# Channel loop of a gated attention and S4 backward kernel: the parameter rows move to the front of an iteration and get a third buffer, the lag sums change their PSUM bank

## The chip, the cores and the metric

The kernel runs on one core of one Trainium2 chip. The metric is the device time of one execution in microseconds (us). Three runs are shown; the profile is of a further execution with a time of its own.

## The reference

The reference is the forward pass of a block and the gradients of all its inputs but one. The block mixes, row by row of x (2048 rows of 576 channels, bfloat16), an attention with 32 heads of width 18 and a convolution of S4 kind with 128 complex states per channel:

```python
x = A_x
g = _sigmoid((x * gate_w).sum(-1, keepdims=True))
a = _A_ref(x, A_wqkv, A_wo)          # softmax attention, 32 heads
b = _B_ref(x, B_A_re, B_A_im, B_B_re, B_B_im, B_C_re, B_C_im, B_log_dt, B_Dskip)
return g * a + (1 - g) * b
...
# _B_ref: K[d,l] = Re sum_n C[d,n] exp(dt[d] A[d,n] l) dB[d,n];  y = causal convolution of K and u, + u * Dskip
_out, _vjp = jax.vjp(_f, A_x, A_wqkv, A_wo, B_A_re, B_A_im, B_B_re, B_B_im, B_C_re, B_C_im, B_log_dt, B_Dskip, gate_w)
```

So thirteen outputs are written: the result, and the gradients of x, the two attention weights, six S4 matrices of 576 x 128, two vectors of the S4 part and the gate.

## The kernel before, in words

The program has four stages that follow each other: projections and preparation, attention forward and backward (8 groups of 4 heads), the channel loop, and a final stage of weight gradients and row-wise outputs. Only the channel loop is changed. It starts at about 2141 us of the profiled execution and ends at about 2587 us.

**The channel loop** (lines 1412 to 1470) does the S4 forward and backward for 576 channels in 18 blocks of CB = 32. It is a software pipeline: iteration i finishes block i, runs the first half of the state scan of block i+1, prepares block i+2 (called sb) and loads for block i+3 (called mb). The order of the instructions is written out by hand on every engine, and SyncE's DMA queue is one of these engines: what stands first in the code is issued first, and an instruction that waits holds up all that stand behind it on its engine.

In one iteration, in the order of the code:

- `scan` (710, on DVE): seven steps over the states of two blocks at once. The first operation of a step multiplies the state by the parameter rows (`tz<-HG,par`, 727). Before it `scan_open` (704) casts the first column out of UV. In iteration i the second of the two chains needs the rows of block i+1.
- `rw1`, `rw2` (744, 751, DVE): products over the whole scan, which read the parameter rows of block i for the last time and leave Rw.
- `m_sum(sb)` (637, PE): four pairs of small matmuls that sum skewed rows (skw) into 32 columns of PSUM, the lag sums, `misc<-sel,skw`. `m_fin(sb)` (642, ACT) copies them out, the third copy into `dDs_row`.
- `m_part(mb)` (611): 32 matmuls (`psM<-xs,gyp`), two copies to mst on ACT (621), and two stores of 288 KB to the DRAM tensor Md_d (622). `m_load(mb+1)` (604) then loads xs (1 MB) and gyp.
- `turn_e(sb, 0)` (655): transposes of the first half of the basis E1n, copied to E1e by ACT.
- `k0(i+1)`, `k0_out` (761, 772): a column sum on PE, a copy K0c on ACT, a store of 8 KB to Kp_d (776). `t0_load(i+1)` (848) reads 1 MB back from Kp_d as T0w (854), so it waits for that store.
- `uv(sb, 0)`, `t0(i)`: matmuls. `m_skw(mb)` (629): four loads of 64 KB (635) that read Md_d with a skew.
- `turn_e(sb, 1)`, then **`load_par(sb)`** (668): three loads of 64 KB, each of 512 rows of 128 bytes, that bring the parameter rows of block i+2. There are two buffers (tag par), and so the rows of block i+2 take the buffer of block i.
- `ybp(i, 0)`, `ybp(i, 1)` (787, PE): matmuls on Rw. Around them `load_en(mb, 0)` and `load_en(mb, 1)` (678): two loads of 1 MB of E1n, each into the buffer that `ybp(i, h)` has just read. `uv(sb, 1)` stands between them.
- `prep_rx` (ACT), `load_rx` every second iteration (RXn, two loads of 256 KB in rows of 128 bytes), `yd_out` (ACT, and every second iteration a store of 512 KB in rows of 128 bytes).
- `pairs1`, `pairs2` (DVE products pq, summed by PE into PSUM with `psum`, 813), `wk_cast(sb)` (ACT, reads the parameter rows), `sums` (841: ACT copies the 384 columns out as `m<-misc`, 843; GpSimd combines them).

**The two banks of sums.** misc2 holds two PSUM tiles of one bank each (lines 1370 to 1373). The bank of block b is b % 2. Columns 0 to 383 take the pair sums of `psum`, 384 to 415 the lag sums (`dkp`, 624), 416 to 447 those of `k0`. `dkp(b)` uses the other bank, (b + 1) % 2. In iteration i the lag sums of block i+2 so fall into bank (i+1) % 2, which is the bank of block i-1, whose pair sums ACT copies out at the end of iteration i-1. In the built program the first matmul of the lag sums waits for that copy, although the two touch other columns; the copies and matmuls of one bank wait for each other as a whole.

**Memory.** The parameter rows lie in a pool on the right side that is opened near the end of the attention stage. `dDs_row` (1347) is one row of 576 float32 in a pool of the channel stage; the final stage converts it to bfloat16 (1634).

Of the kernel before, what the change touches and what calls it, by code (L numbers as in the profile page):

```python
# [11 lines left out]
BF = mybir.dt.bfloat16  # L12
F32 = mybir.dt.float32
# [4 lines left out]
P = 128  # L18


def build(tc, aps, dbg_aps=None, stages=("s1", "attn", "post", "s4", "final")):
# [40 lines left out]
    with ExitStack() as gctx:  # L62
# [559 lines left out]
            Q["mdma"](Md_d[d0 + u * 16:d0 + (u + 1) * 16].rearrange("(q g) t w -> (g t) q w", g=4), mst)  # L622

        def dkp(b):
            return Q["misc2"][(b + 1) % 2][:, 12 * CB:13 * CB]

        skws = {}

# [39 lines left out]
        def load_par(b, dma=nc.sync.dma_start):  # L668
            if b == NBLK - 1:
                par = Q["pw"].tile([P, XB, NCOL], BF, tag="RX", bufs=2, name="par_l").bitcast(F32)[:, 0:12, :]  # L670
            else:
                par = Q["pl"].tile([P, 12, CB], F32, tag="par", bufs=2, name="par")
            blk(b)["par"] = par
            for s_ in range(2):
                dma(par[:, s_:8:2, :], par_d[:, 0:4, b * CB:(b + 1) * CB])
            dma(par[:, 8:12, :], par_d[:, 4:8, b * CB:(b + 1) * CB])
# [58 lines left out]
        def cast1(b, nm, s_):  # L735
            B_ = blk(b)
            HGv = B_["HG"].rearrange("p (r s) k c -> p r s k c", s=2)
            B_[nm] = Q["pw"].tile([P, 2, NS, CB], BF, tag=nm, name=nm)
            nc.scalar.copy(B_[nm], HGv[:, :, s_, ::-1, :])
# [602 lines left out]
        if "s4" in stages:  # L1342
            s4c_cm = tc.tile_pool(name="s4c", reuse_waits="tile", bufs=1)
            s4c = s4c_cm.__enter__()
            SS = Q["SS"] = s4c.tile([P, 6, D], F32, name="SS")
            CK = Q["CK"] = s4c.tile([P, 2, 2, D], BF, name="CK")
            dDs_row = Q["dDs_row"] = s4c.tile([1, D], F32, name="dDs_row")
            ones_f = s4c.tile([P, 1], BF, name="ones_f")
            nc.vector.memset(ones_f, 1.0)

            with ExitStack() as ctx:
                pc = ctx.enter_context(tc.tile_pool(name="s4l", reuse_waits="tile", bufs=1))
                pw = Q["pw"] = Q["en", 2] = ctx.enter_context(tc.tile_pool(name="s4lw", reuse_waits="tile", bufs=1))
                Q["ple"] = ctx.enter_context(tc.tile_pool(name="s4le", reuse_waits="tile", bufs=1))
                pps = Q["ps"] = ctx.enter_context(tc.tile_pool(name="s4lps", reuse_waits="tile", bufs=1, space=bass.MemoryType.PSUM))
                pidx_i = pc.tile([P, 1], mybir.dt.int32, name="pidx_i")
                nc.gpsimd.iota(pidx_i, pattern=[[0, 1]], base=0, channel_multiplier=1)
                l0col = pc.tile([P, 1], F32, name="l0col")
                nc.vector.tensor_copy(l0col, pidx_i)
                l1col = pc.tile([P, 1], F32, name="l1col")  # L1360
                nc.vector.tensor_scalar(l1col, l0col, 1.0, None, op0=A.add)
                sel = pc.tile([P, NSUB], F32, name="sel")
                nc.gpsimd.memset(sel, 1.0)
                nc.gpsimd.affine_select(out=sel, in_=sel, compare_op=A.is_ge, fill=0.0,
                                        base=0, pattern=[[-SUB, NSUB]], channel_multiplier=1)
                nc.gpsimd.affine_select(out=sel, in_=sel, compare_op=A.is_ge, fill=0.0,
                                        base=SUB - 1, pattern=[[SUB, NSUB]], channel_multiplier=-1)
                Q["l0col"], Q["l1col"], Q["sel"] = l0col, l1col, sel
                Q["psM"] = lambda: pps.tile([P, 4, P], F32, tag="bk", bufs=4, name="psM")
                misc2 = Q["misc2"] = []  # L1370
                for u in range(2):
                    m_u = pps.tile([P, 512], F32, tag=f"misc{u}", name=f"misc{u}")
                    misc2.append(m_u)

                ctx.enter_context(tc.manual_schedule(engines={mybir.EngineType.PE, mybir.EngineType.Activation, mybir.EngineType.DVE, mybir.EngineType.Pool}))
                dve_copy = nc.vector.tensor_copy
                KH = NS // 2 + 1
                with tc.manual_schedule(engines={mybir.EngineType.SP}):
                    prep_rx(0, dve_copy)
                    load_en(2, 0)  # L1380
                    wk_cast(0)
                    k0(0)
                    k0_out(0)
                    t0_load(0)
                    turn_e(0, 0, 0, 4, dve_copy)
                    m_sum(0)
                    m_fin(0)
                    uv(0, 0)
                    prep_rx(1, dve_copy)
                    load_rx(1)  # L1390
                    turn_e(0, 1, 0, 4, dve_copy)
                    m_part(1, 0)
                    m_part(1, 1)
                    m_skw(1)
                    m_load(2)
                    uv(0, 1)
                    turn_e(1, 0, 0, 4, dve_copy)
                    scan_open(0)
                    scan((0, 1, KH, 0), (0, 1, KH, 1))
                    turn_e(1, 1, 0, 4)  # L1400
                    m_sum(1)
                    m_fin(1)
                    load_en(2, 1)
                    uv(1, 0)
                    m_part(2, 0)
                    m_part(2, 1)
                    m_skw(2)
                    uv(1, 1)
                    m_load(3)
                    prep_rx(2)  # L1410
                    wk_cast(1)
                    for i in range(NBLK):
                        nx = i + 1 < NBLK
                        mb = i + 3 if i + 3 < NBLK else None
                        sb = i + 2 if i + 2 < NBLK else None
                        if nx:
                            scan_open(i + 1)
                            scan((i, KH, NS, None), (i + 1, 1, KH, None))
                        else:
                            scan((i, KH, NS, 0), (i, KH, NS, 1))  # L1420
                        rw1(i)
                        rw2_open(i)
                        rw2(i)
                        if sb is not None:
                            m_sum(sb)
                            m_fin(sb)
                        if mb is not None:
                            m_part(mb, 0)
                            m_part(mb, 1)
                            if mb + 1 < NBLK:  # L1430
                                m_load(mb + 1)
                        if sb is not None:
                            turn_e(sb, 0, 0, 4)
                        if nx:
                            k0(i + 1)
                        if nx:
                            k0_out(i + 1)
                        cast1(i, "hR", 0)
                        nc.scalar.copy(Q["CK"][:, :, :, i * CB:(i + 1) * CB], BK[i]["UV"][:, :, CDK:CDK + 2, :])
                        if sb is not None:  # L1440
                            uv(sb, 0)
                        t0(i, 0)
                        t0(i, 1)
                        if nx:
                            t0_load(i + 1)
                        cast1(i, "gR", 1)
                        if mb is not None:
                            m_skw(mb)
                        if sb is not None:
                            turn_e(sb, 1, 0, 4)  # L1450
                            load_par(sb)
                        ybp(i, 0)
                        if mb is not None:
                            load_en(mb, 0)
                        if sb is not None:
                            uv(sb, 1)
                        ybp(i, 1)
                        if mb is not None:
                            load_en(mb, 1)
                            prep_rx(mb)  # L1460
                            if mb % 2 == 1 and mb + 1 < NBLK:
                                load_rx((mb + 1) // 2)
                        yd_out(i, 0)
                        yd_out(i, 1)
                        pairs1(i)
                        pairs2(i)
                        if sb is not None:
                            wk_cast(sb)
                        sums(i)
                        BK.pop(i)  # L1470
# [298 lines left out]
```

## Time and profile before

| what | value |
|---|---|
| median of three runs | 2766.22 us (2761.52 to 2767.05) |
| profiled execution, time / span | 2764.32 us / 2762.6 us |
| busy in the span: PE, DVE, ACT, POOL | 88%, 83%, 85%, 62% |
| granted TensorE clock | 0.952 |
| start of an iteration's scan (cast out of UV), i = 0 and i = 17 | 2141.5 us, and 2544.5 us for the last block (a scan is opened an iteration ahead) |
| DVE waits for the parameter rows | 39.0 us, 15 times, 5.3 us the longest |
| PE waits for the copy `m<-misc` before the lag sums | 20.5 us, 16 times |

The profiled execution took 1.7 us more than its span, and 1.9 us less than the median. Times in the text are microseconds from the start of the span. A row of the timeline has the start, the time taken, the engine (SPq is SyncE's DMA queue), the line, the operation with output and input, and in brackets the idle time before it and what ended that. A row of the waits has the engine and line that waited, on what, the sum, how often and the longest.

### The profile page before, as it was taken

Reading aid. Unit: us, or ns where it says so; the run is one execution under the profiler, and the core shown is the slowest. Engines: PE = TensorE matmul, PEld = TensorE weight load, DVE = VectorE, ACT = ScalarE, POOL = GpSimd, SP = SyncE. Lnnn points to the kernel's source line nnn. Section 1 sums busy time; section 2 is a strip of 40 time slices with the busy share of each in tenths; the row PEclk is TensorE's granted clock in tenths of the full one; section 3 lists DMA queues with packets and bytes.
Section 4 is the critical chain, followed back from the end, with each engine's and each line's share of the span. In section 5 each row is a group of like instructions: output and inputs, shape, how many; then the busy total and the mean of one; then the engine's idle time right before and its main releaser. Section 6 shows DMA issues by size and latency. Waiting matters only on the chain. (4 is left out here: it accounts for less than half of the span.)

```text
span 2762.6 us, 70109 instructions
## 1 busy us (share of the span) xinstructions
PE 2430.1 (88%) x27411; PEld 1159.8 (42%) x27411; DVE 2301.0 (83%) x4141; ACT 2360.2 (85%) x2744; POOL 1715.3 (62%) x2667
## 2 busy tenths in 40 slices
PE   8898889898899898889898899898886888888789
PEld 4433333333333333333333333332324788887557
DVE  5649999999899998899999999998973888889944
ACT  5489999999999999999999999999963788887121
POOL 0278878888988888788888888879411133332010
PEclk9889999999999999999999999999966899999899
DMA  7647799989889888988997897796789889885996
GB/s 226 181 108 153 156 173 172 159 159 190 155 163 177 169 157 169 169 163 156 179 166 152 162 183 156 152 190 146 139 165 209 214 239 246 221 239 166 249 261 133
DMA packets 1268279, 491.96 MB, mean 178 GB/s; under 512 B 1161765, under 2 KB 1238166, under 8 KB 1259242
## 3 DMA queue, kind: packets, MB, share of 16 engines
q1 hardware_dynamic: 1231466, 414.96, 73.3%
q0 software_dynamic: 23120, 59.76, 8.6%
q10 hardware_dynamic: 13360, 12.75, 1.6%
q8 instruction: 215, 3.52, 0.6%
q14 instruction: 118, 0.97, 0.1%
HBM read 146.86 MB, written 98.52 MB: 89 GB/s over the span
## 5 line engine op out<-in xcount | busy, mean ns | idle before, releaser
L1321 DVE TENSOR_TENSOR ds<-ps_P,PT 128x512 bf16<-128x512 f32 x2048 | 1311.0, 682 | 128.1 <-PE ps_P L30 87.8
L1316 ACT ACTIVATE eb<-ps_P 128x1024 bf16<-128x1024 f32 x1024 | 1100.9, 1075 | 38.2 <-PE ps_P L30 38.0
L1311 ACT ACTIVATE PT<-ps_P 128x1024 bf16<-128x1024 f32 x1024 | 1106.2, 1081 | 19.9 <-PE ps_P L30 18.5
L30 PE MATMUL ps_P<-dOaT,VaT_g 32*128 32x512 bf16 x2048 | 582.0, 390 | 29.7 <-DVE ds L1321 14.5
L502 POOL TENSOR_TENSOR et<-eG,eT 128x448 f32<-128x448 f32 x576 | 542.2, 961 | 10.7
L30 PE MATMUL ps_P<-QaT_g,KaT_g 32*128 32x512 bf16 x2048 | 403.1, 385 | 137.4 <-ACT PT L1311 124.7
L30 PE MATMUL ps_P<-KaT_g,QaT_g 32*128 32x512 bf16 x2048 | 407.9, 391 | 1.2 <-ACT eb L1316 0.6
L30 PEld LDWEIGHTS <-KaT_g 32*128 32x128 bf16 x2048 | 147.4, 91 | 466.8 <-issue 451.6
L502 POOL TENSOR_TENSOR Eo<-et,et 128x448 bf16<-128x448 f32 x288 | 326.9, 1135 | 20.8
L845 POOL TENSOR_TENSOR SS<-m 128x96 f32<-128x96 f32 x18 | 91.0, 5053 | 340.6 <-ACT m L843 285.9
L30 PEld LDWEIGHTS <-QaT_g 32*128 32x128 bf16 x2048 | 116.3, 91 | 286.7 <-issue 264.3
L30 PE MATMUL accV<-eb,dOa 128*32 128x512 bf16 x2048 | 186.3, 397 | 27.2 <-ACT eb L1316 27.0
L30 PE MATMUL accO<-PT,Vtok_g 128*32 128x512 bf16 x2048 | 207.2, 394 | 0.0
L30 PE MATMUL accK<-dsT,Qtok_g 128*32 128x256 bf16 x4096 | 163.6, 281 | 16.5 <-DMA dsT<-ds 14.7
L30 PE MATMUL accQ<-ds,Ktok_g 128*32 128x512 bf16 x2048 | 161.2, 393 | 2.1 <-DVE dvacc L1079 2.0
L30 PEld LDWEIGHTS <-Vtok_g 128*32 128x32 bf16 x2048 | 52.7, 93 | 222.2 <-issue 222.2
L1030 DVE COPY dsT<-turn_p 128x1024 bf16<-128x1024 bf16 (+1 forms) x216 | 138.7, 642 | 2.7 <-PE turn_p L1025 2.7
L1025 PE MATMUL turn_p<-ident_bf,ds 128*128 128x128 bf16 x1664 | 134.8, 224 | 1.5 <-DVE gb L1097 0.8
L666 ACT COPY E1e<-etp 128x1024 bf16<-128x1024 bf16 x132 | 124.5, 1040 | 5.2 <-PE etp L665 5.0
L727 DVE TENSOR_TENSOR tz<-HG,par 128x256 f32<-128x256 f32 (+1 forms) x245 | 92.6, 412 | 39.0 <-DMA par<-par_d 39.0
L502 POOL TENSOR_TENSOR et<-eT 128x32 f32<-128x32 f32 (+3 forms) x288 | 115.9, 422 | 11.4
L30 PEld LDWEIGHTS <-Qtok_g 128*32 128x32 bf16 x4096 | 88.0, 97 | 81.0 <-issue 61.0
(268 smaller groups left out, 3628.1 us busy)
## 6 DMA issues: line engine op xcount, KB each, us to landing
E_d<-Eo POOLq DMA_DIRECT2D x144, 256.0 KB, 3.3
E1n<-E_d SPq DMA_DIRECT2D x32, 1024.0 KB
xs<-xb_d SPq DMA_DIRECT2D x18, 1024.0 KB
T0w<-Kp_d SPq DMA_DIRECT2D x18, 1024.0 KB
Md_d<-mst SPq DMA_DIRECT2D x36, 288.0 KB
dsT<-ds SPq DMA_TRANSPOSE x512
dqkv_d<-dtk POOLq DMA_DIRECT2D x96, 72.0 KB, 4.3
skw<-Md_d SPq DMA_DIRECT2D x72, 64.0 KB
```

Source lines behind the costliest of these rows:

```text
L30: return nc.tensor.matmul(out, lhsT=lhsT, rhs=rhs, start=start, stop=stop, **kw)
L502: nc.gpsimd.tensor_tensor(out, a, b, op=op)
L666: copy(E_[:, 4 * q:4 * q + 4], pt_)
L727: nc.vector.tensor_tensor(tz[x], HG[:, :, k - 1, :].unsqueeze(1).to_broadcast([P, 2, n, CB]), ZZ, op=A.mult)
L845: nc.gpsimd.tensor_tensor(o_[:, :, 0], m4[:, :, 0], m4[:, :, 3], op=A.subtract)
L1025: nc.tensor.transpose(pt_[:, x, qb, :], t_[:, qb * P:(qb + 1) * P], ident_bf)
L1030: (nc.scalar.copy if NTOT <= now[0] < NTOT + OFF else nc.vector.tensor_copy)(o_(), pt_[:, x:x + n])
L1311: nc.scalar.activation(U["PT"][i, j // 2], ps, ACT.Exp)
L1316: nc.scalar.activation(e, ps, ACT.Exp)
L1321: nc.vector.tensor_tensor(U["ds"][i][:, j, :], ps, U["PT"][i, j // 2][:, j % 2, :], op=A.mult)
```

## The change

Four edits and nothing else:

- `dkp(b)` uses bank b % 2. The lag sums of block i+2 fall into bank i % 2, whose pair sums of block i-2 were copied out in iteration i-2.
- The parameter rows have three buffers. The rows of block i+2 take the buffer of block i-1.
- `load_par(sb)` stands before `turn_e(sb, 0)` and behind `m_load(mb + 1)`. It still loads block i+2 in iteration i. For the last block, whose rows lie in a buffer of RX, it stands behind the matmuls of `t0(i, 1)`.
- `dDs_row` is bfloat16, which takes half its room.

```diff
         def dkp(b):
-            return Q["misc2"][(b + 1) % 2][:, 12 * CB:13 * CB]
+            return Q["misc2"][b % 2][:, 12 * CB:13 * CB]
...
-                par = Q["pl"].tile([P, 12, CB], F32, tag="par", bufs=2, name="par")
+                par = Q["pl"].tile([P, 12, CB], F32, tag="par", bufs=3, name="par")
...
-            dDs_row = Q["dDs_row"] = s4c.tile([1, D], F32, name="dDs_row")
+            dDs_row = Q["dDs_row"] = s4c.tile([1, D], BF, name="dDs_row")
...
                         if sb is not None:
+                            if sb + 1 < NBLK:
+                                load_par(sb)
                             turn_e(sb, 0, 0, 4)
...
                             t0_load(i + 1)
+                        if sb == NBLK - 1:
+                            load_par(sb)
                         cast1(i, "gR", 1)
...
                             turn_e(sb, 1, 0, 4)
-                            load_par(sb)
                         ybp(i, 0)
```

In the order of the built program the four compute engines issue the same operations in the same order as before. On SyncE's queue an iteration read Md_d, Md_d, xs, gyp, Kp_d, T0w, four skw, three par, two E1n, and then RXn or yd_d; it now reads Md_d, Md_d, xs, gyp, three par, Kp_d, T0w, four skw, two E1n, and then RXn or yd_d.

## The prediction

> **What bounds the kernel now.** I read the page first, for the wait that the change is aimed at. The chain of work that ended last reaches back only to 2573 us, so the loop has to be read from its own windows. The page's group of the scan's first operation:
>
> ```profile
> L727 DVE TENSOR_TENSOR tz<-HG,par 128x256 f32<-128x256 f32 (+1 forms) x245 | 92.6, 412 | 39.0 <-DMA par<-par_d 39.0
> ```
>
> DVE idles 39.0 us ahead of it, all of it for the parameter rows. Next the waits between 2150 and 2590 us:
>
> ```profile
> DVE tz L727 <- DMA par<-par_d: 39.0, 15, 5.3
> PEld misc L30 <- ACT m L843: 22.5, 15, 2.6
> PE misc L30 <- ACT m L843: 20.5, 16, 2.5
> DVE HG L708 <- ACT UV L702: 13.2, 9, 4.5
> ```
>
> Both waits that the change attacks are there: 2.6 us an iteration on DVE, 1.3 us on PE (PEld is the same wait, seen by the weight load). If DVE set the pace, 39 us would be at stake. So the third view is the busy time by windows of two iterations each, columns PE, PEld, DVE, ACT, POOL, then clock, DMA share and GB/s:
>
> ```profile
> 2188.00:2238.00 50.00, 43.61 (x763) 40.97 (x761) 42.78 (x104) 40.03 (x63) 8.71 (x4) 0.93 0.89 239
> 2238.00:2288.00 50.00, 44.89 (x792) 42.09 (x790) 44.11 (x105) 42.76 (x66) 19.70 (x4) 0.93 0.91 238
> 2288.00:2337.00 49.00, 43.69 (x762) 41.06 (x760) 42.33 (x104) 40.61 (x64) 20.52 (x4) 0.90 0.91 244
> ...
> 2440.00:2492.00 52.00, 44.23 (x785) 41.15 (x783) 43.87 (x105) 41.47 (x64) 12.02 (x4) 0.97 0.86 229
> 2521.00:2545.00 24.00, 20.42 (x361) 19.87 (x359) 21.96 (x54) 19.96 (x31) 8.38 (x2) 0.93 0.40 130
> ```
>
> DVE is busy 22 us of 25, but the 16 DMA engines as a mean are busy 0.86 to 0.91 of it: 22.4 us of every iteration. Only in the last window, where the big loads have ended, are they at 0.40, and there an iteration takes 24 us. To see where the DMA engines idle, the DMA view of 2288 to 2338, 40 slices of 1.25 us:
>
> ```profile
> DMA  2896999998999999983038979999999499999850
> GB/s 59 295 419 214 206 170 400 400 413 334 215 198 231 283 293 223 223 153 56 0 52 262 400 232 216 237 396 413 419 319 150 71 232 298 340 229 236 167 95 0
> ```
>
> and SyncE's queue over the same stretch:
>
> ```profile
> 2305.13 0.38 SPq L776 DMA_DIRECT2D Kp_d<-K0c  x1
> 2313.22 0.32 SPq L854 DMA_DIRECT2D T0w<-Kp_d  x1
> 2313.63 2.49 SPq L635 DMA_DIRECT2D skw<-Md_d  x4
> 2316.22 0.96 SPq L675 DMA_DIRECT2D par<-par_d  x2
> 2317.22 0.52 SPq L676 DMA_DIRECT2D par<-par_d  x1
> 2317.97 1.51 SPq L684 DMA_DIRECT2D E1n<-E_d  x2
> ...
> 2326.83 1.95 SPq L622 DMA_DIRECT2D Md_d<-mst  x2
> ```
>
> The deep hole, at 2311 to 2314, is the same every iteration: Kp_d is issued at 2305.1, its packets run last in the queue (2309.9 to 2312.2), and T0w, which reads them back, may be issued only at 2313.2. Around it the queue is full. So the loop is a train of transfers of about 25 us with one hole in it, and the par wait is the place where DVE meets this train: the rows are issued at 2316.2, run behind T0w and skw, and DVE starts at 2320.45. Taking the rows out of DVE's way doesn't shorten the train.
>
> **What the Trainium skill says.** DMA: Bandwidth & Descriptors, Queues, rings and completion order: on each DMA engine the descriptors of an issuing engine's queue are consumed in ring order. The trace agrees: T0w's packets run from 2314.2 to 2317.6, skw's from 2317.2 to 2318.9, E1n's from 2319.4. Same page, Specifications: transfers under 512 B do not reach line rate. The 128-byte packets of these rows take 13 ns each here, the 8 KB packets of E1n 318 ns: 9.8 against 25.8 bytes per ns. Same page, Anatomy of one DMA: completion costs most of a fixed 2 us, written for the GpSimd path; here the T0w issue comes 0.6 to 1.0 us after Kp_d's last packet. PSUM, section PSUM bank collisions raise a hardware error: two engines must be kept apart by bank and quadrant, not by address. The trace agrees: the lag sums wait for a copy of other columns.
>
> **The change part by part.**
>
> *Rows earlier.* The three loads are 1536 packets, 1536 x 13.2 ns / 16 = 1.3 us of the DMA engines. Moved from behind skw to ahead of Kp_d they leave the train as long as it was: E1n starts when it did, Kp_d, T0w and skw run 1.3 us later. On SyncE the three issues (1.5 us) pass Kp_d, T0w and skw; Kp_d was issued 4.7 us before its first packet and so loses nothing; T0w is not needed for another 15 us. The third buffer makes the load wait for block i-1's rows, read an iteration before: no wait. The rows then land about 5 us before DVE wants them, so the 39.0 us go. What is late next is UV (13.2 us, unchanged, since it comes from Rw through PE and ACT), and on PE skw: over 13 iterations of the trace its last packet plus 0.9 us lies 1.3 to 5.4 us ahead of the lag sums, median 2.9. It lands 1.3 us later now. The first half of E1n is as near, -0.5 to 4.7 us ahead of its transposes, median 1.6. So the engines can get ahead of the train by about 1.5 to 2 us, then they meet skw or E1n.
>
> *What that lead brings.* First, less idle time of the DMA engines outside the Kp_d hole. From all six windows (also 0.88 of 51, 0.87 of 52) the idle sum is 5.5 + 4.5 + 4.4 + 6.1 + 6.8 + 7.3 = 34.6 us in 12 iterations, 2.9 each. Windows put on five more or less whole holes (2311 to 2314 and the like) give 2.94, 1.74, 1.66, 2.45, 3.11, a mean of 2.4, that stays. Of the other 0.5 us, 14 x 0.5 = 7 us, a part comes from late engines: E1n's issue at 2446.5 waits for ybp, which waits for Rw, and the queue runs dry for 0.9 us; Md_d waits for mst at 2352. The rest (behind RXn, behind yd_d) is the queue's own. I take 4 us, ends 0 and 7. Second, the lead is cashed once at the end. After the last E1n load (2521) the engines set the pace: the scan of i = 15 waits 0.66 us for rows, its lag sums 1.23 us on the bank, and both have the lead of 2 us behind them: 0.7 + 1.2 + 2 = 3.9. The wall there is skw of block 17: last packet 2519.4, so 2519.4 + 1.3 + 0.9 = 2521.6 against lag sums that started at 2526.1, a room of 4.5. I take 4.4 of it, since the copies of ACT behind the lag sums also gain; ends 1 and 5. The final stage keeps what the loop gives: its first load, x_tok, waited for PE's yp until 2563.8, and SyncE's queue and PE follow from there.
>
> *Lag sums in the other bank.* No operation is added. PE no longer waits 1.3 us an iteration, and ACT, which waits 1.15 us for the lag sums and 0.65 and 0.35 us for psM, gets about 1.5 us back. The pair sums of block i now meet the lag sums of i+2 in one bank, some 20 us after ACT copied these: no wait. Inside the train both are cover for PE and ACT, not time; they are part of the lead counted above.
>
> *The bfloat16 row.* The third copy of m_fin takes 0.24 us with 1 x 32 elements in either type; 0, with ends of -1 and +1 us in all. Other addresses of the pools change a few waits between stages; the trace can't price that: -1 to +1.
>
> **Sum.** 2764.3 (the profiled time) - 4 - 4.4 = 2755.9. The median of the runs lies 1.9 us higher, so 2757.8; I say 2758.
>
> **Rivals.** *The engines set the pace.* DVE is busy 21.96 us in the window of i = 15 with 1.9 us of waits. With the rows there, an iteration would take 22 plus the 0.8 us of UV waits, 22.8 instead of 25.3: 14 x 2.5 = 35 us less. Against it stands the train: 22.4 us busy and 2.4 us hole are 24.8, so at most 0.5 us of 2.5 can be had. For it: DMA busy time has waits in it (T0w's packets take 406 ns on average, E1n's 318 at best). Half of it would be 18 to 20 us: 2747, with an end at 2740.
> *The wait only moves.* skw or E1n take the place of the rows at once, and PE's wait passes on to DVE through UV: 0 to 4 us less, 2764.
> *Slower.* T0w and skw are 1.3 us later in each iteration while nothing behind them is earlier. Where skw becomes the last to arrive, m_part, mst and Md_d follow it, and the train waits for Md_d. From skw to Md_d: 0.9 us landing, 1.1 lag sums, 2.1 psM, 0.9 + 0.6 copies on ACT, 1.1 issue and first packet: 6.7 us, against 6 us of E1n and 2.3 us of RXn or yd_d that run meanwhile. It decides when more than 1.6 us come on top, as where PE runs slowly (PE clock 0.55 at 2311 to 2314). At 0.5 us in 14 iterations: +7, 2773.
> That the edit does nothing is excluded: the built order has the rows ahead of Kp_d.
>
> **Chances.** Measured against the median, about 0.2% (5.5 us) is what can be told from no change. The train with a lead (2750 to 2762): 0.55, nine in ten of it faster by over 0.2%. The engines (2740 to 2750): 0.12, faster. The wait only moves (2761 to 2768): 0.21, no change. Slower (2770 to 2778): 0.12. Faster 0.50 + 0.12 = 0.62, same 0.05 + 0.21 = 0.26, slower 0.12. Leaving out most of the slower case and the far end of the engines' one, the range is 2743 to 2768; the likeliest case alone has 2750 to 2762.
>
> **What would show it.** Right: the group of tz has no wait for par; par stands at the end of xs and gyp in the queue; T0w comes 1.3 us later after Md_d; DMA share of a window of two iterations stays at 0.88 to 0.92; the lag sums show waits on skw instead of `m`; two iterations take 49.5 to 50.5 us. Wrong: two iterations in under 48 us with a DMA share over 0.93 would say that the engines had set the pace; over 51.5 us with PE waiting for skw in most iterations, the slower case; an unchanged loop with UV waits of over 30 us, the moved wait.

## The result and the profile after

| what | before | after |
|---|---|---|
| median of the runs taken side by side (22 each) | 2761.68 us (2747.59 to 2767.05) | 2751.74 us (2745.86 to 2760.89) |
| ratio after / before, 95% interval | | 0.9972 [0.9959, 0.9985] |
| profiled execution, time / span | 2764.32 / 2762.6 us | 2746.14 / 2744.4 us |
| first scan (cast out of UV) to first ps_dwq of the final stage | 445.6 us | 433.5 us |
| final stage from there | 175.5 us | 176.5 us |
| one iteration, T0w issue to T0w issue, mean of 13 | 25.36 us | 24.81 us |
| DMA engines busy / idle in it | 22.47 / 2.89 us | 22.82 / 1.99 us |
| last of these T0w issues to the last scan | 52.3 us | 45.5 us |

DMA busy is the sum of all packet times over 16 engines, idle is the rest of the iteration. The ratio is that of the means; it is worth 7.7 us less, with 4.1 to 11.3 as its ends, and the medians stand 9.9 us apart. The two profiled executions differ by 18.2 us, and that is not the change alone: 7.1 us of it lie ahead of the first scan, where both kernels do the same work and the granted clock was 0.96 before and 0.97 after. That point falls anywhere from 2134.4 to 2152.1 us in the kernels of this study. The loop itself is 12.1 us shorter in this pair, with a clock of 0.93 in both.

The waits of the kernel after between 2143 and 2583 us (engine and line, on what, sum, times, longest). The stretch begins 8.6 us behind the first scan's start, as 2150 does in the kernel before; the wait of 11 to 12 us at that start, which both have, stays out:

```profile
DVE HG L708 <- ACT UV L702: 38.8, 14, 4.7
PEld misc L30 <- DMA skw<-Md_d: 31.4, 42, 3.3
ACT RX L646 <- PE misc L30: 30.7, 13, 4.0
PE misc L30 <- DMA skw<-Md_d: 25.3, 29, 3.2
...
PE yp L30 <- DVE Rw L754: 15.1, 2, 7.8
PEld L665 <- DMA E1n<-E_d: 9.8, 14, 1.5
```

The 39.0 us that DVE waited for the rows are gone, and so are PE's 20.5 us for the copy `m`. In their place PE waits 25.3 us for skw, and DVE waits 38.8 us for UV where it waited 13.2. DVE's two waits together are 52.2 us before and 38.8 after, 13.4 less: about what the loop became shorter by. PE's waits are in part exchanged, with this line of the kernel before beside the lines above:

```profile
PE yp L30 <- DVE Rw L754: 28.4, 13, 7.6
```

`m` and Rw together are 48.9 us before, skw and Rw 40.4 after.

Windows of two iterations as in the prediction, four of six, columns PE, PEld, DVE, ACT, POOL, then clock, DMA share and GB/s:

```profile
2182.00:2233.00 51.00, 46.77 (x825) 43.78 (x823) 45.65 (x109) 43.40 (x69) 15.22 (x4) 0.93 0.89 234
2233.00:2282.00 49.00, 43.82 (x778) 40.59 (x776) 43.28 (x105) 40.91 (x65) 15.25 (x4) 0.93 0.93 243
2282.00:2332.00 50.00, 44.76 (x777) 41.83 (x775) 43.57 (x104) 41.09 (x65) 15.30 (x4) 0.90 0.92 239
...
2431.00:2480.00 49.00, 44.85 (x788) 41.94 (x786) 43.75 (x106) 41.55 (x65) 15.23 (x4) 0.93 0.93 243
```

DMA is now at 0.89 to 0.93; two iterations take 49 to 51 us where they took 49 to 52. DVE is still idle for 5 to 6.5 us of each window. The DMA view of 2282 to 2332, slices of 1.25 us:

```profile
DMA  0899999999999999993049888999986999999980
GB/s 13 288 413 286 284 347 387 387 349 213 180 207 269 284 229 223 188 192 34 5 111 387 336 239 270 328 341 380 326 193 93 224 291 341 216 236 181 185 79 7
```

One hole in each iteration, as before (slices 18 to 20, and the edges), and little else: the dips that stood between E1n and Md_d are smaller. And SyncE's queue in that stretch:

```profile
2282.45 0.33 SPq L854 DMA_DIRECT2D T0w<-Kp_d  x1
2282.83 2.51 SPq L635 DMA_DIRECT2D skw<-Md_d  x4
2285.44 0.88 SPq L684 DMA_DIRECT2D E1n<-E_d  x2
...
2298.14 1.16 SPq L675 DMA_DIRECT2D par<-par_d  x2
2299.35 0.56 SPq L676 DMA_DIRECT2D par<-par_d  x1
2300.01 0.46 SPq L776 DMA_DIRECT2D Kp_d<-K0c  x1
2306.78 0.33 SPq L854 DMA_DIRECT2D T0w<-Kp_d  x1
```

The rows are issued behind gyp and land long before the scan; Kp_d is right behind them, and T0w still has to wait 6.3 us for it. From DVE's rows of the timeline, the scan that begins at 2282:

```profile
2281.99 0.23 DVE L708 CAST HG<-UV 128x128 f32<-128x128 bf16 x1 [2.82 <-ACT UV L702]
2282.14 0.75 DVE L727 TENSOR_TENSOR tz<-HG,par 128x256 f32<-128x256 f32 x2
```

`tz` starts while the cast ahead of it ends, with no wait for rows. What is late is the cast's own input.

### The profile page after: what moved, and what is told of

Its sections match the earlier page's. It is cut to its first block, busy times and chain, and to the rows that moved or that the text cites. A ratio compares the mean times of both kernels' runs of the same rounds, so it can differ in the third digit from the quotient of the medians.

```text
span 2744.4 us, 70052 instructions
## 1 busy us (share of the span) xinstructions
PE 2416.0 (88%) x27411; PEld 1154.1 (42%) x27411; DVE 2301.1 (84%) x4141; ACT 2356.5 (86%) x2744; POOL 1718.6 (63%) x2667
## 5 line engine op out<-in xcount | busy, mean ns | idle before, releaser
L30 PE MATMUL accK<-dsT,Qtok_g 128*32 128x256 bf16 x4096 | 162.5, 280 | 16.4 <-DMA dsT<-ds 14.7
L1025 PEld LDWEIGHTS <-ds 128*128 128x128 bf16 x1664 | 97.3, 99 | 49.7 <-issue 49.7
```

The costliest lines, as they stand in the source:

```text
L30: return nc.tensor.matmul(out, lhsT=lhsT, rhs=rhs, start=start, stop=stop, **kw)
L1025: nc.tensor.transpose(pt_[:, x, qb, :], t_[:, qb * P:(qb + 1) * P], ident_bf)
```

## The experiments

Each edit is shown against the kernel after, and each ratio is to the kernel before, run beside it on the same chip. The runs stand in three groups on two chips, so groups are compared through these ratios. The iteration is T0w issue to T0w issue, the mean of 13, as in the table above.

**Which edit does it? The bank alone (e1_bank_only).** The rows go back to their old place and to two buffers; the bank and the bfloat16 row stay.

```diff
-                par = Q["pl"].tile([P, 12, CB], F32, tag="par", bufs=3, name="par")
+                par = Q["pl"].tile([P, 12, CB], F32, tag="par", bufs=2, name="par")
...
-                            if sb + 1 < NBLK:
-                                load_par(sb)
...
-                        if sb == NBLK - 1:
-                            load_par(sb)
...
                             turn_e(sb, 1, 0, 4)
+                            load_par(sb)
```

> Only the lag sums change their bank (and the one-row buffer its type); the parameter rows stay where they were, with two buffers. Theory (the train of transfers sets the pace, the engines' lead is what is gained): DVE still waits some 39 us for the rows, PE's wait of 20 us for the copy of the pair sums is gone, the copies on ACT come about 1.5 us earlier, two iterations still take 50 to 51 us: 0 to 3 us less than before, a ratio of 0.999 to 1.000. Rival (the bank is what pays): 6 to 8 us less, a ratio of 0.997 to 0.998.

Measured: 1.0002 [0.9986, 1.0019], 25.46 us an iteration. Its waits between 2152 and 2592 us:

```profile
DVE tz L727 <- DMA par<-par_d: 33.3, 14, 3.7
...
DVE HG L708 <- ACT UV L702: 20.0, 16, 4.0
```

PE no longer waits for `m` (0.6 us, once), DVE still meets the train at the rows, and no gain is seen; the interval leaves room for one of up to 4 us. The 1.3 us an iteration that PE gets back don't shorten the train.

**The rows alone (e2_rows_only).** All of the change but the bank.

```diff
-            return Q["misc2"][b % 2][:, 12 * CB:13 * CB]
+            return Q["misc2"][(b + 1) % 2][:, 12 * CB:13 * CB]
```

> Only the rows move, with the third buffer; the lag sums stay in the other bank. Theory: no wait of DVE for the rows, PE waits for the copy of the pair sums as before (some 20 us), so PE has about 1.2 us less room ahead of skw and gets less lead; the most of the gain stays: 4 to 7 us less than before, a ratio of 0.9975 to 0.9985. Rival (the bank is what pays): no change, 1.000.

Measured: 0.997 [0.9953, 0.9988], 24.96 us an iteration. Its waits between 2146 and 2586 us:

```profile
DVE HG L708 <- ACT UV L702: 39.8, 16, 4.5
...
PEld misc L30 <- ACT m L843: 23.1, 13, 2.5
PE misc L30 <- DMA skw<-Md_d: 19.2, 15, 4.3
```

As far as the runs can tell, the whole effect comes from the rows' place. The bank's wait is back beside that for skw, and the ratio can't be told from that of the kernel after (0.9972).

**The third buffer (e7_two).** As after, with two buffers.

```diff
-                par = Q["pl"].tile([P, 12, CB], F32, tag="par", bufs=3, name="par")
+                par = Q["pl"].tile([P, 12, CB], F32, tag="par", bufs=2, name="par")
```

> The changed kernel with two buffers of rows instead of three, loaded at the same early place: the load of block i+2 then waits for DVE's last product with the rows of block i (wb), and Kp_d, T0w and skw stand behind it on SyncE's queue. In the changed kernel's trace wb ends 0.4 to 1.2 us before the load is issued. Theory (only the place in the queue pays): 0 to 3 us more than the changed kernel, a ratio of 0.997 to 0.998. Rival (the third buffer pays): SyncE is held up, Kp_d comes late and the hole grows by 1 us or more an iteration: 1.001 and above.

Measured: 0.9967 [0.9952, 0.9981], 24.80 us. With two buffers the load waits for the scan of block i to have read its rows; in the trace of the kernel after that reader, `wb`, ends 0.2 to 2.4 us before the load is issued in 11 of 15 iterations, and 0.5 to 4.1 us behind it in the other four. In e7 SyncE waits 2.5 us for `wb` between 2160 and 2480 us, in two iterations. The third buffer brings nothing that these runs show, and the lead it covers is thin.

**What a transfer costs ahead of Kp_d, and what in the hole (e4_dup, e5_hole).** Three copies of the same rows into a scratch tensor in device memory, which nobody reads: in e4 right behind the rows, in e5 between Kp_d and T0w.

```diff
+        def copy_par(b):
+            dst = pc_d[b].rearrange("p (r c) -> p r c", r=12)
+            for s_ in range(2):
+                nc.sync.dma_start(dst[:, s_:8:2, :], par_d[:, 0:4, b * CB:(b + 1) * CB])
+            nc.sync.dma_start(dst[:, 8:12, :], par_d[:, 4:8, b * CB:(b + 1) * CB])
...
                                 load_par(sb)
+                                copy_par(sb)    # e4
...
                             k0_out(i + 1)
+                        if sb is not None and sb + 1 < NBLK:
+                            copy_par(sb)        # e5
```

> The changed kernel, and behind the three loads of rows in every iteration of the loop but the last three copies of the same rows to a scratch tensor in DRAM, ahead of the Kp_d store; nobody reads them. Theory (train): each iteration gets longer by what these packets take on the DMA engines, 1.3 us if they cost what the loads do, up to 3 us since they also write rows of 128 bytes to DRAM; 15 iterations, 20 to 45 us more than the changed kernel, a ratio to the kernel before of 1.004 to 1.014. Rival (engines): nothing waits for these copies, the time stays that of the changed kernel, 0.997.

> The three copies of rows to a scratch tensor again, now behind the Kp_d store and ahead of T0w. Theory (the train has a hole there): the copies take some 2.1 us an iteration on the DMA engines (what they cost ahead of Kp_d), the hole is 2.4 to 2.7 us, so most of them is hidden: 0 to 10 us more than the changed kernel, a ratio to the kernel before of 0.997 to 1.0005. Rival (a transfer costs the same wherever it stands in a full queue): as ahead of Kp_d, 1.006.

Measured: e4 1.0064 [1.0039, 1.0089] and 26.95 us an iteration, 2.14 more than after. e5 0.9987 [0.9975, 0.9999] and 25.26 us, 0.45 more. The copies make the DMA engines 1.51 us busier an iteration in e4 (24.33 us against 22.82) and 1.41 in e5 (24.23). In e4 0.63 us of idle time come on top; in e5 0.96 us of idle time go. A lower clock has a share in e4: over the 13 iterations it was 0.88 there, 0.92 in e5 and 0.93 in the kernel after, and PE is busy 23.05, 22.74 and 22.60 us an iteration. That is 0.45 us of the 2.14 at most; the contrast with e5 is larger. The waits of e4 between 2153 and 2593 us:

```profile
PE misc L30 <- DMA skw<-Md_d: 52.2, 19, 5.8
DVE HG L715 <- ACT UV L709: 51.4, 15, 4.9
```

The same packets cost 2.14 us in the train and 0.45 us in the hole. That is the train's signature: the copies count in full where the queue is full, and for a third of their packet time where it stands empty. It also shows where the wait moved: with skw later, PE waits 52.2 us for it in place of 25.3, and DVE 51.4 us for UV in place of 38.8.

**Where is the engines' floor? (e3_no_xs).** The loads of xs are left out of the loop: the lag sums reuse the block loaded last, only gyp is loaded.

```diff
-                                m_load(mb + 1)
+                                xss[mb + 1] = xss[mb]
+                                nc.sync.dma_start(Q["gyp2"][(mb + 1) % 2][:, 0:SUB, :].rearrange("p t c -> p (t c)"), gyb_d[mb + 1])
```

> The changed kernel without the 1 MB load of xs for blocks 4 to 17 (the lag sums of these blocks are made from block 3's xs, so the gradients that use them are not the reference's); all other transfers and all instructions of the compute engines stay. Theory (train): the train of an iteration gets some 4.8 us shorter, and the engines set the pace, 22 to 23 us instead of 24.8: 14 iterations, 25 to 39 us less than the changed kernel, a ratio to the kernel before of 0.983 to 0.988, and the waits for skw are gone. Rival (engines): they waited for no xs, so the time stays that of the changed kernel, 0.997.

Measured: 0.9828 [0.981, 0.9846], 22.16 us an iteration, no wait for skw or E1n left. Its windows of two iterations:

```profile
2250.00:2294.00 44.00, 42.20 (x786) 39.70 (x784) 43.72 (x106) 41.26 (x66) 15.22 (x4) 1.00 0.79 226
2294.00:2338.00 44.00, 42.18 (x761) 39.84 (x758) 42.30 (x104) 40.24 (x63) 15.17 (x4) 0.96 0.77 220
```

DVE is busy 42.3 to 43.7 us of 44 and DMA falls to 0.77 to 0.79. So 22.2 us is about what the engines need where this load doesn't bind; the kernel after is 2.65 us an iteration above that. Not all of this is the train's: the clock over the 13 iterations was 0.98 here and 0.93 in the kernel after, where PE alone is busy 22.60 us an iteration (21.34 here). With PE's times of the kernel after at most 2.2 us are to be had.

**Closing the hole (e6_fill, run again as e6_again).** If the train is the bound, independent transfers between Kp_d and T0w should shorten it. The rows and skw go there.

```diff
-                            if sb + 1 < NBLK:
-                                load_par(sb)
...
                             k0_out(i + 1)
+                        if sb is not None and sb + 1 < NBLK:
+                            load_par(sb)
+                        if mb is not None:
+                            m_skw(mb)
...
-                        if mb is not None:
-                            m_skw(mb)
```

> The changed kernel with the rows and the four skw loads put behind the Kp_d store and ahead of T0w, so that they run while T0w waits for Kp_d. Theory (train): the hole of 2.4 us in each iteration is filled with 3 us of work that was in the train anyway, and skw, for which PE waits now, lands 3 us earlier: an iteration takes 22.8 to 23.3 us instead of 24.8 (from 22.8 on the engines set the pace), 14 iterations, 20 to 28 us less than the changed kernel, a ratio to the kernel before of 0.987 to 0.990. Rival (engines): only the skw wait goes, 0.995 to 0.997.

> The same kernel as the version with rows and skw in the hole, run again beside the next two so that they can be compared: a ratio to the kernel before of 0.986 to 0.990.

Measured: 0.9877 [0.9849, 0.9905] with 23.52 us an iteration, then 0.9917 [0.9896, 0.9938] with 23.70. The medians are 2736.62 us beside 2766.83 of the kernel before, and 2743.99 beside 2767.29. The two intervals touch only at their ends, so the gain is 0.8 to 1.2%. Both iterations are longer than the 22.8 to 23.3 us that were expected, and the second ratio misses its range of 0.986 to 0.990. No other kernel of the study that computes everything is measurably faster. Its DMA view of 2300 to 2350:

```profile
DMA  1999999992399999999469999999989889989918
GB/s 50 253 387 360 393 393 400 366 206 47 57 232 295 358 210 223 184 185 143 114 112 382 400 400 413 406 369 235 172 160 276 196 177 223 249 171 166 168 14 201
```

The hole of slices 18 to 20 of the kernel after is one of about two half-empty slices here (19 and 20). The dip at slices 9 and 10 falls where an issue of RXn takes 7.08 us. DMA idle time is 1.00 us an iteration (1.29 in the second run) in place of 1.99. The wait of T0w for Kp_d, in SyncE's waits of the kernel after

```profile
SPq L854 <- DMA Kp_d<-K0c: 88.2, 14, 7.0
```

and of e6_fill:

```profile
SPq L854 <- DMA Kp_d<-K0c: 0.5, 1, 0.5
```

A part of that wait has become issue time: to get the four skw loads out takes SyncE 2.5 to 3.0 us in the kernel after and 5.0 to 7.2 us here, ahead of T0w. What PE waits for last now is E1n; the waits of e6_fill between 2148 and 2588 us:

```profile
DVE HG L708 <- ACT UV L702: 26.5, 12, 4.4
...
PEld L665 <- DMA E1n<-E_d: 19.6, 9, 4.1
...
PE etp L665 <- DMA E1n<-E_d: 15.2, 8, 3.5
```

**Only skw in the hole (e8_skw_hole).**

```diff
                             k0_out(i + 1)
+                        if mb is not None:
+                            m_skw(mb)
...
-                        if mb is not None:
-                            m_skw(mb)
```

> The changed kernel with the four skw loads alone put behind Kp_d and ahead of T0w; the rows stay ahead of Kp_d. Theory (train): 1.7 us of the hole are filled and skw lands 3.3 us earlier; SyncE needs 2.5 us to issue the four ahead of T0w, within the time that Kp_d waits in the queue: 18 to 24 us less than the changed kernel, a ratio to the kernel before of 0.988 to 0.991. Rival (it was the rows in the hole that paid in the version with both): 0.995 to 0.997.

Measured: 0.9922 [0.9897, 0.9947], 23.67 us, a little less gain than expected. PE waits 19.4 us for E1n here. It can't be told from e6_again, so skw alone fills the hole about as well; whether the rows add something can't be told.

**T0w later still (e9_between, e10_last).** Since T0w is wanted late and E1n is late, T0w goes between the halves of E1n (e9) or behind both (e10), on top of e6_fill.

```diff
-                        if nx:
+                        if nx and mb is None:
                             t0_load(i + 1)
...
                             load_en(mb, 0)
+                            t0_load(i + 1)      # e9
...
                             load_en(mb, 1)
+                            t0_load(i + 1)      # e10
```

> Rows and skw behind Kp_d as in the version that fills the hole, and T0w put between the two loads of E1n, so that the first half of E1n, for which PE waited 15 us in that version, lands one load (3.3 us) earlier. Theory (train, with E1n as the load that comes last): the E1n waits go, an iteration takes 22.5 to 23 us instead of 23.5, 7 to 14 us less than that version, a ratio to the kernel before of 0.983 to 0.986. Rival (T0w was the cover under which E1n's issue waits for PE's ybp): the queue runs dry before E1n, no gain or a loss, 0.987 to 0.993.

> As the last one, with T0w behind both loads of E1n. Theory (train): both halves of E1n land earlier, but T0w waits on SyncE for ybp of the second half too; 5 to 14 us less than the version that fills the hole, 0.983 to 0.986. Rival (cover lost): both issues of E1n wait for PE with nothing queued, 2 us an iteration more than that version, 0.993 to 1.000.

Measured: e9 0.9918 [0.9897, 0.9939] and 23.95 us, e10 0.9909 [0.988, 0.9938] and 23.69 us. Both miss: no gain over e6_again (0.9917), which ran beside them, and no loss either. In e9

```profile
DVE tz L727 <- DMA par<-par_d: 12.3, 10, 2.6
```

and in e10

```profile
DVE tz L727 <- DMA par<-par_d: 19.9, 10, 3.8
...
PEld L665 <- DMA E1n<-E_d: 11.0, 10, 2.6
```

the rows, which these two kernels load behind Kp_d, are late again. E1n's wait (19.6 us in e6_fill) is 6.8 us in e9 and 11.0 in e10, and another load takes its place. Whether a third order gets below 23.5 us was not tried.

## Why the prediction held, step by step

**The bound: right.** The loop is a train of transfers. The copies cost 2.14 us ahead of the hole (e4) and 0.45 us in it (e5), taking xs out lets the engines run at 22.16 us (e3), and filling most of the hole gives 1.1 to 1.3 us an iteration (e6). "Taking the rows out of DVE's way doesn't shorten the train" is what was seen: 39 us of wait went, and 8 us of time.

**Rows earlier: right in direction, two terms wrong.** The rows' wait is gone, the stretch from Md_d's first packet to Kp_d's last has grown from 8.5 to 10.0 us (1.3 was said), and skw is next. "What is late next is UV (13.2 us, unchanged)" failed: it is 38.8 us. The prediction looked at UV's inputs, and not at what DVE does once it is no longer held at the rows: it comes to the cast early and waits there for PE, which stands in its own queue behind lag sums that wait for skw. In the iteration that ends with the scan at 2282, the lag sums wait for skw until 2262.6 and again until 2263.7, the transposes wait 0.96 us more for E1n (2267.6), and from 2268.6 on neither PE nor ACT has a wait up to UV: its matmuls start at 2278.7, ACT's copies of it end at 2282.0, and DVE, idle for 2.82 us, casts. The runs move with it: without a wait for skw or E1n UV is waited for 9.3 us (e3), with 25.3 us for skw 38.8 (after), with 52.2 us 51.4 (e4). In e6_fill and e8, where skw is early (1.2 us at most) and PE waits 15.2 and 19.4 us for E1n, it is 26.5 and 24.3. So UV shows the wait for whichever load comes last. The second wrong term is what the rows cost in their new place, below. The prediction had named UV waits over 30 us as the sign of the rival "the wait only moves", but with an unchanged loop; the wait did move and the loop is shorter by 2%, so that sign alone doesn't tell the two apart. That rival's 0 to 4 us lie just below the interval of 4.1 to 11.3.

**The third buffer: no wait, but idle.** Two buffers have no wait that matters either (e7).

**The hole stays: right, but its size was not.** From Kp_d's last packet to T0w's first the DMA engines lose 1.64 us an iteration before and 1.53 after, measured packet by packet. The 2.4 us of the prediction came from windows that took in the hole's edges.

**Less DMA idle elsewhere: mis-sized.** "I take 4 us, ends 0 and 7." The iteration is 0.55 us shorter, 13 x 0.55 = 7.1 us, just past the far end. Outside the hole there were 2.89 - 1.64 = 1.25 us of idle time, and not the 0.5 that the prediction thought were to be had. Idle fell by 0.90 us an iteration: by 0.40 between T0w and E1n's end, 0.19 from there to Md_d, 0.19 between Md_d and Kp_d, 0.11 in the hole (the parts are sums of packet times in stretches, so good to 0.1). Late issues may be part of it: RXn's wait for ACT's yd fell from 14.6 to 4.6 us. Against it, DMA busy time rose by 0.35 us an iteration, 22.47 to 22.82, which the prediction had at 0 ("they leave the train as long as it was"). The rows' own packets account for it: behind xs and gyp they took 18.2 ns as a mean in place of 13.8, so 1.75 us in place of 1.33. Each of the 13 iterations shows it (16.7 to 20.5 ns after, 12.9 to 14.7 before), and so do e1, with the rows at their old place (13.6 as a mean), and e2, with the rows moved alone (18.5), while the other 128-byte packets took 14.6 in place of 14.5. Why the rows' packets take longer there is open.

**The lead at the end: mis-sized.** 4.4 was taken out of 1 to 5; from the last T0w issue of the train to the last scan it is 6.8 us. So the trace has 7.1 + 6.8 = 13.9 us where the sum said 8.4; 1.8 us of that are given back ahead of the first T0w counted, 1.0 in the final stage. The runs say 7.7 (4.1 to 11.3), so one pair of profiles overstates the change; e2 and e7, with loops of 434.9 and 435.1 us, have 8.3 and 9.1 us by their ratios. The total agrees with the runs; the split between the two terms can't be settled finer than some 3 us. So it is luck in part that 8.4 us came so near to 7.7: in the trace both terms are larger than said, and the hole, the idle time and the rows' packets behind them were each off. The figure of 2758 also stood on a median of 2766.22 us of three runs; from the 2761.68 of the 22 runs the same sum gives 2753.3, against 2751.74 measured.

**The bank and the bfloat16 row: right.** Both are cover; e1 measures them together at 1.0002.

**The rivals.** The engines' floor is real (22.16 us measured at the higher clock of e3, 22.8 said), but the train is not let down to it. The packet times given for it don't hold: in the trace of the kernel before T0w's mean is 364 ns and that of E1n 359 (309 as a median), where the prediction has 406 and 318; the slow packets of 8 KB are those of xs, some 560 ns. The slower case, skw holding up Md_d, did not come: PE waits for skw by up to 3.2 us, and yet the DMA engines lose only 0.01 us an iteration between E1n's end and Md_d's first packet. Nor does it come past the point that the prediction named, with the copies' 1.5 us more ahead of skw (e4): nothing is lost there either, and of the 0.63 us of new idle time 0.49 lie between Md_d's first packet and Kp_d's last, where the copies stand.

## What to carry to other kernels

A wait on a load can be a place in a queue and not a price: sum the transfers of one iteration and their holes first, and if they make up the period, removing a wait buys only what the lead lets the queue avoid. Then look for a store that is read back at once: the wait for its landing is a hole, and independent transfers issued into it cost little (0.45 us for 1.41 of packets here), where swapping loads in the stretch behind it gained nothing (e9, e10). Price a moved transfer at its new place: the same rows took 1.33 us in one and 1.75 in the other. After each such move name the next load to be late, since here the wait went from the rows to skw, to E1n, and back to the rows.

## What was not expected of the hardware

An issue can last long on SyncE. In e6_fill, at 2304.8 us, the first load of RXn took 0.57 us to issue and the second 7.08, of equal size and with no wait named; both stand behind T0w and E1n. The four skw loads, which take 2.5 to 3.0 us to get out behind T0w in the kernels before and after, take 5.0 to 7.2 us behind Kp_d and the rows in e6_fill. It happens without these changes too: the two Md_d issues take 1.3 to 6.8 us in the kernel before and 1.8 to 5.6 in the kernel after. Issues this long were in no step of the prediction, and no run here takes them apart.

The small packets' own time is not fixed: the mean of the rows' packets rose from 13.8 to 18.2 ns with nothing but their place changed. The Trainium skill (DMA: Bandwidth & Descriptors, Specifications) has transfers under 512 B below line rate. That agrees: 128 bytes in these times are 7.0 to 9.3 bytes per ns, against some 20 for the 8 KB packets of the loop (407 to 411 ns as a mean). That the loss also depends on the place in the queue is only seen here.
